# Linear attention with a two-layer PReLU block: batch 0 laid out as 96 partitions of 6 tokens, three stores on another queue, and steps re-placed

## The chip, the cores and the metric

The kernel runs on one core of a Trainium2 chip. The metric is device time in microseconds (us) of one execution; the median of several runs is compared. One execution is also taken by the hardware profiler, and all trace rows come from that one. The engines are TensorE (PE, with its weight loads shown as PEld), VectorE (DVE), ScalarE (ACT), GpSimd (POOL) and SyncE (SP). All of them take their instructions in order. SP, ACT and POOL issue the DMAs.

## The reference

For each of 8 batches and 8 heads (576 tokens, head size 64), linear attention without a softmax, an RMS norm over the head size, and then a two-layer block over all 4608 tokens:

```python
kv = einsum('bhsd,bhse->bhde', k, v)           # 64 x 64 per head
out = einsum('bhsd,bhde->bhse', q, kv)
out = out / sqrt(mean(out * out, -1) + 1e-6) * g_norm
x = out.transpose(0, 2, 1, 3).reshape(4608, 512)
h = x @ w_in                                    # 512 -> 2048
y = (max(h, 0) + alpha * min(h, 0)) @ w_out     # 2048 -> 512
```

Inputs and output are fp32; the kernel computes with fp16 operands and fp32 sums.

## The kernel before

**Blocks and batches.** The 4608 tokens are worked in nine blocks of 512 (`w`), so a block reaches over the edge of a batch of 576. Heads go in four pairs (`j`), since two heads of 64 fill 128 rows. Attention of block `w+1` is computed while block `w` goes through the two-layer block. There are five attention steps per pair. `step_t` transposes q on PE into `qt_ps` and copies it to `qt_sb`. `step_kv` sums k's product with v over the batch's tokens into `kv_ps`, and DVE masks it to `kv_sb`. `step_ot` multiplies the two into `ot_ps`, and ACT squares that. `ssq_mm` sums the squares by a matmul with `mask16`, and ACT makes `rstd`. `norm` (DVE) writes `xt`. `step_ssq` is the last two together.

**Tokens in partitions.** A batch of 576 tokens is loaded as 128 partitions of 4 tokens (`load_main`, fp32 in memory to an fp16 stage `kst`, `qst`, `vst`) and a remainder of 64 tokens (`load_rem`, into `ksb`, `qsb`, `vsb`). Both go through POOL's queue, which casts. The remainder's upper 64 partitions are zeroed once in each of three buffers (`nc.vector.memset(t[nm][REM:P, n - 1, :, :], 0.0)`, line 123), so that all five transposes (line 238) and all five kv matmuls (line 256) of a pair have 128 rows. k and q of the stage are brought into the order of tokens by `regroup` (DVE whole, line 149, or ACT by pairs, `regroup_pair`, line 147).

**Start.** Batch 0 comes in halves. The first four heads of q and k are loaded as fp32 by SP and ACT (`early_half`), cast by DVE and ACT (`cast_pair`, line 520). The rest comes through POOL: three remainders, then v's first half, q's and k's second halves, v's second half, the five pieces of `w_in`, and then batches 1 and 2 and `w_out` in turn. Ten matmuls of `keep_warm` occupy PE until data comes, and three more stand ahead of the first `step_kv`. `alpha_ps` (line 545) transposes the row of alphas in fp32: it is the only matmul with 16 rows.

**Two-layer block.** `m1_group` multiplies `xt` by a column group of `w_in` (four matmuls of 128x512 into one of three banks h0, h1, h2, line 320); `m1_evac` empties the bank by an ACT step (`m_sb`, line 327) and a DVE step (`gt`, line 331), after which it can be filled again. Block 0 multiplies by `w_out` directly (`y_mm`, line 345). Later blocks use a scheme with seven half-size products in place of eight (`prod_mm`, line 468), whose operands are sums of `gt` tiles (`s_sum`) and of weights (`w_sum`). Each block has 16 units `u`, in each of which one `m1_group`, seven products of the block before, and the attention steps due at that unit are issued.

**Order.** The program order of each engine is written out by hand (a manual schedule), so an engine that waits holds everything behind it. Block 2's attention, issued in block 1, follows the table `ATT_1`, all later ones `ATT_AT`. The PSUM tiles come from few banks: h0 to h2, `y`, `s`, `q` and two of `o`; a step waits until its bank's last reader is done. In block 1, ACT copies q of batch 3 in units 12 to 15 (`REG_1`), and k in units 0 and 1 of block 2.

**Stores.** `y_out` copies a finished 128x512 tile to `y_sb` on ACT, and `store_rows` issues its DMA on SP, split where a run of partitions ends.

Of the kernel before, what the change touches and what calls it, by code (L numbers as in the profile page):

```python
# [9 lines left out]
FP32 = mybir.dt.float32  # L10
# [7 lines left out]
def kernel(  # L18
# [11 lines left out]
    nc = tc.nc  # L30
# [12 lines left out]
    REM = S - MAIN  # L43
    NT = TPP + 1
    NF = D_FF // P
    NC = D_MODEL // P
    assert NC == NPAIR and 0 < REM < P
    inv_d = 1.0 / D
# [23 lines left out]

    def early_half(eng, nm, tag):
        st32[nm] = w_p.tile([P, H // 2, TPP * D], FP32, name=f"{nm}32", tag=tag)
        eng.dma_start(
            out=st32[nm][:],
            in_=srcs[nm][0, 0 : H // 2, 0:MAIN, :].rearrange("h (p t) d -> p h (t d)", t=TPP),
        )

    early_half(nc.sync, "q", "wsum2")  # L80
    early_half(nc.scalar, "k", "wsum4")

# [12 lines left out]

    warm16 = const_p.tile([P, W], FP16, name="warm16")
    nc.vector.memset(warm16[:], 0.5)
# [8 lines left out]

    alpha_row = const_p.tile([NF, P], FP32, name="alpha_row")
    nc.sync.dma_start(out=alpha_row[:], in_=moe_alpha[:].rearrange("(g p) -> g p", p=P))
    g2col = const_p.tile([P, 1], FP32, name="g2col")
# [5 lines left out]

    NBUF = 3
    bufs = []
    for i in range(NBUF):
        t = {}
        for nm in ("k", "v", "q"):  # L120
            n = 1 if nm == "v" else NT
            t[nm] = qkv_p.tile([P, n, H, D], FP16, name=f"{nm}sb{i}")
            nc.vector.memset(t[nm][REM:P, n - 1, :, :], 0.0)
        bufs.append(t)
    stages = {}

    def load_main(b, nm, h0, h1):
        st = stages.get((b, nm))
        if st is None:
            st = stage_p.tile([P, H, TPP, D], FP16, name=f"{nm}st", tag=f"{nm}st")  # L130
            stages[b, nm] = st
        nc.gpsimd.dma_start(  # L132
            out=st[:, h0:h1, :, :].rearrange("p h t d -> p h (t d)"),
            in_=srcs[nm][b, h0:h1, 0:MAIN, :].rearrange("h (p t) d -> p h (t d)", t=TPP),
        )
# [15 lines left out]
    def load_batch(b, names=("k", "v", "q")):  # L151
        for nm in names:
            load_rem(b, nm)
            load_main(b, nm, 0, H)

    def regroup_pair(b, nm, j):
        regroup(b, nm, 2 * j, 2 * j + 2, nc.scalar)
# [33 lines left out]

    HH = H // 2
    for nm in ("q", "k", "v"):
        load_rem(0, nm)
    load_main(0, "v", 0, HH)
    load_main(0, "q", HH, H)
    ident = const_p.tile([P, P], FP32, name="ident")
    make_identity(nc, ident[:])
    load_main(0, "k", HH, H)
    load_main(0, "v", HH, H)  # L200
    for i in range(len(IN_CUTS) - 1):
# [21 lines left out]
    qts, kvs, xts = {}, {}, {}  # L223

    def pair_cols(b, nm, j):
        def f(t):
            if nm == "v" and t < TPP:
                return stages[b, nm][:, 2 * j : 2 * j + 2, t, :]
            if nm == "v":
                return bufs[b % NBUF][nm][:, 0, 2 * j : 2 * j + 2, :]  # L230
            return bufs[b % NBUF][nm][:, t, 2 * j : 2 * j + 2, :]
        return f

    def step_t(b, j, pool=(ps_s, "s")):
        qs = pair_cols(b, "q", j)
        qt_ps = pool[0].tile([P, NT * P], FP16, name="qt_ps", tag=pool[1])
        for t in range(NT):
            nc.tensor.matmul(  # L238
                out=qt_ps[:, t * P : (t + 1) * P],
                lhsT=qs(t),  # L240
                rhs=ident16[:],
                is_transpose=True,
                start=(t == 0),
                stop=(t == NT - 1),
            )
        qts[b, j] = attn_p.tile([P, S], FP16, name="qt_sb", tag=f"qt{j}")
        if b == 0:
            nc.vector.tensor_copy(out=qts[b, j][:], in_=qt_ps[:, 0:S])
        else:
            nc.scalar.copy(out=qts[b, j][:], in_=qt_ps[:, 0:S])  # L250

    def step_kv(b, j, pool=(ps_s, "s")):
        ks, vs = pair_cols(b, "k", j), pair_cols(b, "v", j)
        kv_ps = pool[0].tile([P, P], FP32, name="kv_ps", tag=pool[1])
        for t in range(NT):
            nc.tensor.matmul(  # L256
                out=kv_ps[:],
                lhsT=ks(t),
                rhs=vs(t),
                start=(t == 0),  # L260
                stop=(t == NT - 1),
            )
        kvs[b, j] = attn_p.tile([P, P], FP16, name="kv_sb", tag=f"kv{j}")
        nc.vector.tensor_mul(out=kvs[b, j][:], in0=kv_ps[:], in1=mask32[:])  # L264
# [84 lines left out]

    store_engines = [(nc.sync,)]  # L350
    store_turn = [0]

    def store_rows(n0, src, c0, c1):
        i = 0
        while i < P:
            b, r = divmod(n0 + i, S)
            if r < MAIN:
                t, p = divmod(r, P)
                cnt = min(P - i, P - p)
                rows = out[b * S : b * S + MAIN, :].rearrange("(p t) m -> t p m", t=TPP)  # L360
                dst = rows[t, p : p + cnt, c0:c1]
            else:
                cnt = min(P - i, S - r)
                dst = out[b * S + r : b * S + r + cnt, c0:c1]
            engs = store_engines[0]
            store_turn[0] += 1
            engs[store_turn[0] % len(engs)].dma_start(out=dst, in_=src[i : i + cnt])
            i += cnt
# [149 lines left out]

    def cast_pair(nm, st, j, eng_copy):
        eng_copy(  # L520
            out=bufs[0][nm][:, 0:TPP, 2 * j : 2 * j + 2, :].rearrange("p t h d -> p h t d"),
            in_=st[:, 2 * j : 2 * j + 2, :].rearrange("p h (t d) -> p h t d", t=TPP),
        )

    cast_pair("q", st32["q"], 0, nc.vector.tensor_copy)
    cast_pair("k", st32["k"], 0, nc.scalar.copy)
    step_t(0, 0, H_POOL)
    cast_pair("q", st32["q"], 1, nc.vector.tensor_copy)
    cast_pair("k", st32["k"], 1, nc.scalar.copy)
    step_t(0, 1, H_POOL)  # L530
# [4 lines left out]
    step_ot(0, 1)  # L535
    regroup(0, "q", HH, H)
    step_t(0, 2, H_POOL)
    step_t(0, 3, H_POOL)
    regroup(0, "k", HH, H)
    ssq_mm(0, 0, Q_POOL)  # L540
    ssq_mm(0, 1)
    norm(0, 0)
    norm(0, 1)
    alpha_ps = ps_h.tile([P, NF], FP32, name="alpha_ps", tag="h0")
    nc.tensor.matmul(
        out=alpha_ps[:], lhsT=alpha_row[:], rhs=ident[0:NF, 0:NF], is_transpose=True,
        start=True, stop=True,
# [4 lines left out]
    )  # L552
    step_kv(0, 2)
    step_kv(0, 3, Q_POOL)
    step_ot(0, 2)
    step_ot(0, 3, (ps_y, "y"))
# [75 lines left out]
    y_run(1, range(12, 16))  # L632
    y_out(ys[1], 0, 1)
    h_turn[0] = 0
    h_tags[0] = ("h0", "h1", "h2")
# [18 lines left out]
    for what, ats in (  # L654
        ("kv", (1, 2, 3, 4)), ("t", (5, 6, 7, 9)), ("ot", (7, 8, 10, 11)), ("ssq", (9, 10, 12, 13))
    ):
        for j, at in enumerate(ats):
            ATT_1.setdefault(at, []).append((what, j))
    ATT = {"t": step_t, "kv": step_kv, "ot": step_ot, "ssq": step_ssq}

    def attention(w, u):
        if w < NW:
            for what, j in (ATT_1 if w == 2 else ATT_AT).get(u, ()):
                if w < B or what in ("ot", "ssq"):
                    if w == 2 and what in ("kv", "ssq"):
                        pool = O_POOL if what == "kv" and j % 2 else Q_POOL
                        (step_kv if what == "kv" else step_ssq)(w, j, pool)
                    elif w == 2 and what == "ot" and j == 2:
                        step_ot(w, j, (ps_y, "y"))
                    else:  # L670
                        ATT[what](w, j)

    REG_1 = {12 + j: (("q", j),) for j in range(NPAIR)}
    REG_AT = {8 + 2 * j + i: ((nm, j),) for j in range(NPAIR) for i, nm in ((0, "q"), (1, "k"))}

    for w in range(1, NW):
        if w + 2 < B:
            load_batch(w + 2)
        for u in range(NF):
            m1_group(w, G_ORDER[u])  # L680
            if w > 1:
                unit_sums(w, u)
            if w == 1 and u == 4:
                regroup(2, "q", 0, H)
            if w == 2 and u == 0:
# [14 lines left out]
            if w == 1:  # L700
                for k in {7: (0,), 9: (1,), 13: (2,)}.get(u, ()):
                    s_sum(1, 1, k)
                    s_sum(1, 2, k)
            if w + 2 < B:
                for nm, j in (REG_1 if w == 1 else REG_AT).get(u, ()):
                    regroup_pair(w + 2, nm, j)
            if w == 2 and u < 2:
                for j in (2 * u, 2 * u + 1):
                    regroup_pair(3, "k", j)
    w = NW - 1  # L710
    store_engines[0] = (nc.sync, nc.scalar)
# [41 lines left out]
```

## Time and profile before

| | before |
|---|---|
| median of 3 runs (lowest, highest) | 298.6 us (297.7, 299.46) |
| the profiled execution | 297.6 us, of which its span 295.8 us |
| mean granted PE clock | 0.998 |
| PE busy, DVE busy, ACT busy, POOL busy | 95%, 75%, 60%, 16% of the span |
| DMA | busy without a break from about 5 to 75 us, then in pieces |
| HBM read, written | 36.71 MB, 9.44 MB |

A row of a timeline has the start in us, the time in us, engine, line and operation, what is written from what is read, the shape, and in square brackets how long the engine stood idle before it and what ended that. "issue" means that it waited for nothing that the profile shows. Rows of equal instructions are merged (`x5`), and the time is then from the first start to the last end. A matmul's time includes its way through the array, so in a run of them the next starts before the last has ended. Lines with L are lines of the kernel before.

### The profile page before, as it was taken

The numbers are of one execution on the slowest core, as the hardware profiler recorded it, in microseconds if no ns is written. First come the engines' busy times: TensorE is split into PE (matmuls) and PEld (weight loads), VectorE is DVE, ScalarE is ACT, GpSimd is POOL, SyncE is SP. The second block draws the span as 40 slices with busy tenths as digits, with TensorE's granted clock in tenths as the row PEclk, the third lists the DMA queues.
The fourth block names the chain that finished last, engine by engine and source line by source line (L and its number), as shares of the span: only waits on it lengthen the run. The fifth ranks groups of instructions, "written<-read, shape, count | busy, mean of one in ns | idle before, by whom it ended". The sixth has DMA issues, their size and how long they took to land.

```text
span 295.8 us, 5159 instructions
## 1 busy us (share of the span) xinstructions
PE 280.1 (95%) x1970; PEld 179.3 (61%) x1970; DVE 221.5 (75%) x419; ACT 176.1 (60%) x307; POOL 45.9 (16%) x64
## 2 busy tenths in 40 slices
PE   6779999998999999999999999999999999999993
PEld 2434454444666677666666677666666666666782
DVE  6559829679587877797778777877887788787861
ACT  3347367499758856775677668765745565433210
POOL 8644344440203120122002000000000000000000
PEclk9999999999999999999999999999999999999999
DMA  7999999999631990199019401110103011201223
GB/s 159 188 205 198 197 201 193 231 208 192 70 38 39 181 159 5 38 160 161 28 38 136 121 2 35 39 54 21 35 8 100 1 38 35 70 3 37 73 78 100
DMA packets 53081, 28.66 MB, mean 97 GB/s; under 512 B 15152, under 2 KB 52544, under 8 KB 53056
## 3 DMA queue, kind: packets, MB, share of 16 engines
q0 software_dynamic: 41376, 17.83, 48.5%
q1 hardware_dynamic: 10368, 9.32, 10.7%
q10 hardware_dynamic: 1312, 1.18, 1.4%
q8 instruction: 15, 0.25, 0.4%
q14 instruction: 10, 0.08, 0.1%
HBM read 36.71 MB, written 9.44 MB: 156 GB/s over the span
## 4 chain that ended last, share of the span: by engine, by line
PE 69%; DMA 18%; ACT 5%; issue 3%; DVE 2%; POOL 1%; DVEq 0%; POOLq 0%; ACTq 0%
PE h_ps L320 31%; PE yY L468 12%; PE yZ L468 10%; PE yX L468 9%; DMA qst<-in_q_dram 6%; DMA vst<-in_v_dram 5%; DMA w_in_sb<-in_moe_w_in_dram 5%; DMA ksb<-in_k_dram 2%; ACT m_sb L327 2%; PE qt_ps L238 2%; PE ssq_ps L294 2%; PE kv_ps L256 2%; PE ot_ps L278 2%; DVE y_sb L495 1%; ACT ksb L147 1%
## 5 line engine op out<-in xcount | busy, mean ns | idle before, releaser
L320 PE MATMUL h_ps<-xt,w_in_sb 128*128 128x512 f16 x576 | 145.3, 379 | 2.0 <-DVE gt L331 1.8
L331 DVE SCALAR_TENSOR_TENSOR gt<-m_sb,beta_sb,h_ps 128x512 f16<-128x512 f32 x144 | 106.9, 746 | 49.5 <-ACT m_sb L327 47.8
L327 ACT ACTIVATE m_sb<-h_ps 128x512 f32<-128x512 f32 x144 | 86.3, 600 | 65.0 <-PE h_ps L320 50.7
L320 PEld LDWEIGHTS <-w_in_sb 128*128 128x128 f16 x576 | 54.3, 98 | 48.3 <-issue 4.4
L468 PEld LDWEIGHTS <-s 128*128 128x128 f16 x512 | 50.1, 98 | 21.6 <-issue 2.5
L468 PEld LDWEIGHTS <-gt 128*128 128x128 f16 x384 | 37.6, 98 | 14.8
L468 PE MATMUL yY<-wsum,s 128*128 128x256 f16 x256 | 36.3, 273 | 0.0
L468 PE MATMUL yX<-w_out_sb,gt 128*128 128x256 f16 x256 | 35.1, 273 | 0.0
L284 ACT ACTIVATE sq_sb<-ot_ps 128x512 f16<-128x512 f32 x36 | 21.5, 605 | 17.5 <-PE ot_ps L278 17.5
L296 ACT ACTIVATE rstd<-ssq_ps,eps_t 128x512 f32<-128x512 f32 x36 | 24.7, 693 | 9.5 <-PE ssq_ps L294 9.5
L304 DVE SCALAR_TENSOR_TENSOR xt<-ot_ps,g2col,rstd 128x512 f16<-128x512 f32 x36 | 26.5, 745 | 4.2 <-ACT rstd L296 4.2
L250 ACT COPY qt_sb<-qt_ps 128x576 f16<-128x576 f16 x28 | 17.6, 641 | 6.0 <-PE qt_ps L238 6.0
L468 PE MATMUL yZ<-w_out_sb,s 128*128 128x256 f16 x128 | 17.5, 272 | 1.2 <-DVE y_sb L495 1.2
L468 PE MATMUL yY<-wsum,gt 128*128 128x256 f16 x128 | 17.6, 273 | 0.0
L468 PE MATMUL yZ<-wsum,s 128*128 128x256 f16 x128 | 17.6, 273 | 0.0
L345 PE MATMUL y<-w_out_sb,gt 128*128 128x512 f16 x64 | 17.1, 379 | 0.1
L132 POOL DMA_DIRECT2D vst<-in_v_dram x9 | 7.9, 876 | 59.3 <-PE kv_ps L256 52.7
L238 PE MATMUL qt_ps<-ident,qsb 128*128 128x128 f16 x160 | 14.1, 225 | 1.6 <-DVE qsb L520 0.9
L294 PE MATMUL ssq_ps<-sq_sb,mask 128*128 128x512 f16 x36 | 13.5, 379 | 1.4 <-ACT rstd L296 0.7
L278 PE MATMUL ot_ps<-qt_sb,kv_sb 128*128 128x512 f16 (+7 forms) x64 | 13.6, 286 | 0.9 <-DVE kv_sb L264 0.7
L256 PEld LDWEIGHTS <-ksb 128*128 128x128 f16 x160 | 11.6, 100 | 4.1 <-issue 1.3
L238 PEld LDWEIGHTS <-qsb 128*128 128x128 f16 x160 | 10.9, 100 | 5.2 <-DVE qsb L520 1.9
(57 smaller groups left out, 226.1 us busy)
## 6 DMA issues: line engine op xcount, KB each, us to landing
out_dram<-y_sb SPq DMA_DIRECT2D x72, 64.0 KB, 2.1
kst<-in_k_dram POOLq DMA_DIRECT2D x7, 512.0 KB, 12.4
qst<-in_q_dram POOLq DMA_DIRECT2D x7, 512.0 KB, 12.7
vst<-in_v_dram POOLq DMA_DIRECT2D x7, 512.0 KB, 12.7
out_dram<-y_sb SPq DMA_DIRECT2D x23, 128.0 KB, 2.0
w_out_sb<-in_moe_w_out_dram POOLq DMA_DIRECT2D x4, 512.0 KB, 16.5
w_in_sb<-in_moe_w_in_dram POOLq DMA_DIRECT2D x3, 512.0 KB, 12.6
out_dram<-y_sb SPq DMA_DIRECT2D x4, 256.0 KB, 6.9
```

What stands on the lines that cost most here:

```text
L238: nc.tensor.matmul(out=qt_ps[:, t * P : (t + 1) * P], lhsT=qs(t), rhs=ident16[:], is_transpose=True, start=(t == 0), stop=(t == NT - 1),)
L250: nc.scalar.copy(out=qts[b, j][:], in_=qt_ps[:, 0:S])
L256: nc.tensor.matmul(out=kv_ps[:], lhsT=ks(t), rhs=vs(t), start=(t == 0), stop=(t == NT - 1),)
L278: nc.tensor.matmul(out=ot_ps[:, n0 - w * W : n1 - w * W], lhsT=kvs[b, j][:], rhs=qts[b, j][:, n0 - b * S : n1 - b * S], start=True, stop=True,
L284: nc.scalar.activation(out=sq[:], in_=ot_ps[:], func=AF.Square)
L294: nc.tensor.matmul(out=ssq_ps[:], lhsT=mask16[:], rhs=sq[:], start=True, stop=True)
L296: nc.scalar.activation(out=rstd[:], in_=ssq_ps[:], func=AF.Abs_reciprocal_sqrt, bias=eps_t[:], scale=inv_d,)
L304: nc.vector.scalar_tensor_tensor(out=xts[w, j][:], in0=ot_ps[:], scalar=g2col[:], in1=rstd[:], op0=ALU.mult, op1=ALU.mult,)
L320: nc.tensor.matmul(out=h_ps[:], lhsT=w_in_blk(c, g), rhs=xts[w, c][:], start=(c == 0), stop=(c == NC - 1),)
L327: nc.scalar.activation(out=m_sb[:], in_=h_ps[:], func=AF.Relu, scale=-1.0)
L331: nc.vector.scalar_tensor_tensor(out=gts[w, i][:, r, :], in0=m_sb[:], scalar=beta_sb[:, g : g + 1], in1=h_ps[:], op0=ALU.mult, op1=ALU.add,)
L468: nc.tensor.matmul(out=bank, lhsT=lhs, rhs=rhs, start=fresh, stop=(c == NK - 1), skip_group_check=True,)
```

## The change

Batch 0 alone is now cut into 96 partitions of 6 tokens (`P0`, `T0`), which has no remainder: its three `load_rem` go, its q and k first halves are loaded by pairs, its second halves and v come in tiles of their own, and its attention steps make six matmuls of 96 rows where they made five of 128. The upper parts of the remainders of batches 1 to 7 are no longer zeroed; their fifth transpose and fifth kv matmul take the 64 rows that hold data. Block 0's three tiles y0, y2 and y1 are stored from POOL's queue. In the first norm chain `alpha_ps` and `beta_sb` come ahead of the norms, `step_kv(0, 2)` uses an h bank and both kv steps come ahead of the second norm. In block 1 the steps of `ATT_1` are moved, the sums of squares alternate between banks q and s, q of batch 3 is copied by DVE at once in unit 15, and the `s_sum` steps are moved. To make room in SBUF, `warm16` and `alpha_row` share buffers with other tiles.

```diff
+    T0 = next(n for n in range(NT, S) if S % n == 0)
+    P0 = S // T0
...
-    early_half(nc.sync, "q", "wsum2")
-    early_half(nc.scalar, "k", "wsum4")
+    early_pair(nc.sync, "q", 0, "wsum2")
+    early_pair(nc.scalar, "k", 0, "wsum4")
+    early_pair(nc.sync, "q", 1, "wsum1")
+    early_pair(nc.scalar, "k", 1, "wsum3")
...
-    warm16 = const_p.tile([P, W], FP16, name="warm16")
+    warm16 = attn_p.tile([P, W], FP16, name="sq_sb")
...
-    alpha_row = const_p.tile([NF, P], FP32, name="alpha_row")
+    alpha_row = ysb_p.tile([P, D_MODEL], FP32, name="y_sb")
...
-            n = 1 if nm == "v" else NT
+            n = 1 if nm == "v" else T0 if i == 0 else NT
-            nc.vector.memset(t[nm][REM:P, n - 1, :, :], 0.0)
...
-    for nm in ("q", "k", "v"):
-        load_rem(0, nm)
-    load_main(0, "v", 0, HH)
-    load_main(0, "q", HH, H)
+    load_half0("v", 0)
+    load_half0("q", 1)
     ident = const_p.tile([P, P], FP32, name="ident")
     make_identity(nc, ident[:])
-    load_main(0, "k", HH, H)
-    load_main(0, "v", HH, H)
+    load_half0("k", 1)
+    load_half0("v", 1)
...
+    def rows(b, t):
+        return P0 if b == 0 else P if t < TPP else REM
+
+    def n_runs(b):
+        return T0 if b == 0 else NT
...
     def step_t(b, j, pool=(ps_s, "s")):
         qs = pair_cols(b, "q", j)
-        qt_ps = pool[0].tile([P, NT * P], FP16, name="qt_ps", tag=pool[1])
-        for t in range(NT):
+        qt_ps = pool[0].tile([P, S], FP16, name="qt_ps", tag=pool[1])
+        c = 0
+        for t in range(n_runs(b)):
+            n = rows(b, t)
             nc.tensor.matmul(
-                out=qt_ps[:, t * P : (t + 1) * P],
+                out=qt_ps[:, c : c + n],
                 lhsT=qs(t),
-                rhs=ident16[:],
+                rhs=ident16[0:n, 0:n],
...
-    store_engines = [(nc.sync,)]
+    store_engines = [(nc.gpsimd,)]
...
-    regroup(0, "q", HH, H)
+    regroup_half0("q")
     step_t(0, 2, H_POOL)
     step_t(0, 3, H_POOL)
-    regroup(0, "k", HH, H)
+    regroup_half0("k")
     ssq_mm(0, 0, Q_POOL)
     ssq_mm(0, 1)
-    norm(0, 0)
-    norm(0, 1)
     alpha_ps = ps_h.tile([P, NF], FP32, name="alpha_ps", tag="h0")
...
-    step_kv(0, 2)
+    norm(0, 0)
+    step_kv(0, 2, H_POOL)
     step_kv(0, 3, Q_POOL)
+    norm(0, 1)
     step_ot(0, 2)
...
     y_out(ys[1], 0, 1)
+    store_engines[0] = (nc.sync,)
...
-        ("kv", (1, 2, 3, 4)), ("t", (5, 6, 7, 9)), ("ot", (7, 8, 10, 11)), ("ssq", (9, 10, 12, 13))
+        ("kv", (1, 2, 3, 4)), ("t", (6, 7, 8, 9)), ("ot", (8, 9, 11, 12)), ("ssq", (10, 11, 13, 14))
...
-                        pool = O_POOL if what == "kv" and j % 2 else Q_POOL
+                        pool = Q_POOL if j % 2 == 0 else O_POOL if what == "kv" else S_POOL
...
-    REG_1 = {12 + j: (("q", j),) for j in range(NPAIR)}
...
-            if w == 1 and u == 4:
-                regroup(2, "q", 0, H)
+            if w == 1 and u in (4, NF - 1):
+                regroup(2 if u == 4 else 3, "q", 0, H)
...
-                for k in {7: (0,), 9: (1,), 13: (2,)}.get(u, ()):
+                for k in {5: (0,), 8: (1,)}.get(u, ()):
...
+                s_sum(1, u + 1, 2)
```

## The prediction

> **What bounds the kernel now.** I read the page's busy times first, then busy time by stage, then the order of time in the two stages where TensorE (PE) is not full.
>
> ```profile
> span 295.8 us, 5159 instructions
> PE 280.1 (95%) x1970; PEld 179.3 (61%) x1970; DVE 221.5 (75%) x419; ACT 176.1 (60%) x307; POOL 45.9 (16%) x64
> ```
>
> Three stages: the start, most of block 1, and a whole block (columns: stretch and length, then busy time and instructions of PE, PEld, DVE, ACT and POOL, PE's granted clock, DMA share, GB/s).
>
> ```profile
> 2.00:17.90 15.90, 12.00 (x62) 5.64 (x63) 8.97 (x27) 5.37 (x10) 12.24 (x19) 1.00 1.28 200
> 54.00:74.00 20.00, 17.25 (x111) 9.07 (x110) 16.03 (x29) 17.18 (x33) 4.68 (x6) 1.00 1.54 203
> 104.77:135.20 30.43, 30.18 (x230) 20.64 (x228) 24.03 (x46) 21.44 (x38) 4.32 (x6) 1.00 0.65 98
> ```
>
> From 74 us on a block of 512 tokens takes 30.4 us, of which PE is busy 30.2: there PE time alone counts, and any added PE time moves the end one for one. Time can be won only ahead of that: in the start (to 17.9) and in block 1 (54 to 75). The start, in order of time:
>
> ```profile
> 10.47 0.58 PE L256 MATMUL kv_ps<-vst,ksb 128*128 128x128 f16 x4 [0.38 <-DMA vst<-in_v_dram]
> 12.95 0.59 PE L294 MATMUL ssq_ps<-sq_sb,mask 128*128 128x512 f16 x2
> 13.47 0.13 PEld L545 LDWEIGHTS alpha_ps<-ident,alpha_row 16*128 16x128 f32 x1 [0.42 <-issue]
> 13.48 0.23 PE L545 MATMUL alpha_ps<-ident,alpha_row 16*128 16x16 f32 x1
> 14.37 1.39 DVE L304 SCALAR_TENSOR_TENSOR xt<-ot_ps,g2col,rstd 128x512 f16<-128x512 f32 x2
> 15.77 0.47 DVE L264 TENSOR_TENSOR kv_sb<-kv_ps,mask 128x128 f16<-128x128 f32 x2
> ```
>
> And the four stalls of block 1, named in brackets:
>
> ```profile
> 57.62 0.45 PE L238 MATMUL qt_ps<-ident,qsb 128*128 128x128 f16 x5 [0.70 <-DVE qsb L149]
> 65.09 0.38 PE L294 MATMUL ssq_ps<-sq_sb,mask 128*128 128x512 f16 x1 [0.56 <-ACT rstd L296]
> 68.68 0.38 PE L294 MATMUL ssq_ps<-sq_sb,mask 128*128 128x512 f16 x1 [0.19 <-ACT rstd L296]
> 74.20 1.02 PE L320 MATMUL h_ps<-xt,w_in_sb 128*128 128x512 f16 x4 [1.50 <-DVE gt L331]
> ```
>
> **Remainders of batches 1 to 7.** The pads that were zeroed are gone, so the fifth of each run of transposes and of kv matmuls now has 64 rows instead of 128. The built program gives these 56 matmuls (7 batches x 4 pairs x 2) an array tile of 64 rows, and all others 128. So PE changes tile 112 times; before it did so only around alpha. Alpha is the trace's one row for this. The second sum of squares starts at 12.95 + 0.59 - 0.38 = 13.16. Its follower could start 0.215 later (four 128x512 take 0.86 in steady state), at 13.38. Alpha started at 13.48, 0.10 late, though the engine waited for nothing ("issue"). Its weight load, which elsewhere starts some 0.2 us before its matmul, started with it: the load was not taken ahead of the change. I price a change of tile at 0.10 us. Bounds: zero, if alpha was late for being fp32 and not for its rows; 0.165, if PE waits for the last matmul to end (0.219 for one 128x128 transpose against its 0.055 spacing: five take 0.44). I take 0.10 because it is the only row with fewer rows.
> Where it lies: 8 matmuls in batch 1's steps (36 to 42 us, PE back to back) and 40 in blocks 2 to 6, all on the path: 48 x 0.20 = 9.6. The 8 of batch 2 lie in block 1, where ACT and DVE set the pace for half of it: 8 x 0.10 = 0.8. Against that 28 transposes are 64 columns instead of 128: 0.027 each at most, -0.75. Sum +9.65, between -0.75 and about +16.5.
> The Trainium skill, page TensorEngine Tiling (Array Packing), section Key Properties, speaks against this change: it says that switching the tiling mode drains TensorE. It gives no price. If a drain means that a matmul's whole latency is exposed, the sum would be the upper bound above; alpha's 0.10 us is less.
>
> **The start.** The three 64-row loads of batch 0 leave Pool's queue, 0.7 to 0.8 us of issue each, and v's first half is issued first instead of fourth. It landed at 10.34 by its semaphore; I expect some 3 us earlier. But PE then stands in its own queue: ten warm-up matmuls (0.427 apart at the start), a transpose, DVE's copy and second cast, another transpose and three warm-ups end near 10.05, because the cast of 96x768 costs about 0.6 where 128x512 took 0.42. So kv starts 0.4 earlier, not 3. Then 12 kv matmuls instead of 10 at 0.107 each cost 0.2; the copies of q and k from the stage have 1536 elements a partition instead of 1024, 0.42 to 0.63 for q (+0.2) and k with 0.84 now (+0.1 to +0.4, I take 0.1 because k lands earlier). Only one norm (0.70) and beta (0.16) are left ahead of kv_sb: 0.86 where 14.45 to 15.77 was 1.32, -0.5. PE's wait there for rstd to leave bank s goes too, since kv takes an h bank. Sum -0.4, range -1.0 to +0.4. The nine memsets (0.27 each) ended at 4.75, before q landed at 5.81, so nothing comes from them; the identity comes some 2 us earlier on Pool, and nobody waits for it. The buffers that warm16 and alpha_row now share come round again only after their last reader. The split q and k loads are hidden by the warm-ups, which end at 6.5; without that cover a later first cast would cost its lateness.
>
> **Block 1.** The 0.70 goes: q of batch 2 landed at 56.85 with 768 KB of stores beside it and is now asked for a unit later. The waits for rstd (0.56 + 0.19) go: there one sum of squares waited until the one before it had left bank q, and now they alternate banks q and s. ACT loses four copies of 0.62 at units 12 to 15. But the last norm is a unit later, so the next block's first group waits for it: rstd 0.7 after the matmul of unit 14, two DVE steps of 0.75 behind it, 0.6 late. And DVE copies batch 3's q (0.69) just ahead of the evacuation that frees the bank for the second group, so of the 1.50 about 0.9 stays. The third pair of s sums (0.42 each) moves from unit 13 into block 2's units 0 and 1, behind those evacuations; the first two move up a unit or two, where DVE idles. The stalls sum to 2.95; less 0.6 and 0.9 that leaves a gain of 1.45. ACT's 2.5 us of copies shorten its other waits for PE's results a little, and I take -1.7 (from -0.5, if DVE's backlog reaches the norms, to -2.6, if only 0.35 stays).
>
> **Stores on Pool.** Six store issues (about 0.75 each) wait for ACT's three copies of y, at 47.6 to 50. Behind them on Pool stand batch 3's loads, which were issued from 42.9. DMA is not empty for this: what was issued by 41 lasts until q of batch 2 lands, now about 52, and then the stores run. q of batch 3 landed at 68.04 and should land near 65; its copy at unit 15 comes near 68. Cost zero; without that cover DVE, and then PE, would wait the difference.
> The Trainium skill, page DMA: Bandwidth & Descriptors, section Issuing engines are not separate DMA queues, says that DMAs of all issuing engines run on the same 16 engines and interleave, so that moving stores saves issue time only. By it q of batch 2 gains nothing from the move; the 0.70 would still go, by the later unit, and the sum is the same.
>
> **Sum.** +9.65 - 0.4 - 1.7 = +7.55 on the profiled execution's 297.6 (span 295.8), 305.1. The median of the runs, 298.6, is 1.0 above that execution: 306.1, I say 306.
>
> **Rivals.**
> The tile change is free, and the edits do what they are for: -0.75 - 0.4 - 1.7 = -2.85, 295.8 at the median. For it: alpha is fp32, one row, and each 64-row weight load could be hidden as the 128-row ones are. Against: its load had no other reason to be late. It decides below 2.85 / 104 = 0.027 us a change (104 = 48 x 2 + 8). By the ends of the start and block 1, the range is 294 to 297.5.
> A change costs about that, 0.02 to 0.04: within the 0.5% (1.5 us) that a measurement of this kernel can tell from no change.
> A change exposes the whole latency, 0.165: 104 x 0.165 = 17.2, less 2.85, +14.3, 313. Against: alpha's 0.10.
> Pool's queue becomes the bound: batch 3's loads behind the stores. It needs q of batch 3 to land after 68.5, over 3 us later than I reckon, and each us after that is one us of PE. With a free tile change it would eat the 2.85 at a landing of 71.4; 4 us beyond that make 302.6. Against: DMA has the stores themselves to do from 52 to 54, when the first of those loads has long been issued.
>
> **Chances.** Forecast, 0.04 to 0.14 a change: 0.58. Whole latency: 0.06. Pool's queue: 0.02. Break-even: 0.06. Free: 0.28. The forecast's own range is 300 to 311 (104 x 0.04 or x 0.14, less 2.85, on 298.6). The range for 8 in 10 must reach into the free case, since that holds over 0.2: 294.8 to 313. Faster 0.28, same 0.06, slower 0.66.
>
> **What would show it.** In the changed profile blocks 2 to 6 take about 31.9 us each instead of 30.4 (8 x 0.19), and weight loads of the 128x64 transposes and of the next matmul start with their matmul and not ahead. If those blocks keep 30.2 to 30.4, the tile change is free and I am wrong by the whole first term. The first group of block 0 should start at 17.5, the four stalls leave 1.6, and q of batch 2 land near 52. A start at 15 or a block 1 without stalls would show that I under-rated those; a DVE copy of q in unit 15 that waits for a DMA would show Pool's queue.

## The result, and the profile after

| | before | after |
|---|---|---|
| median of 4 runs each (lowest, highest) | 298.62 us (297.7, 299.46) | 306.8 us (306.31, 307.55) |
| the profiled execution | 297.6 us, span 295.8 us | 307.55 us, span 305.8 us |
| mean granted PE clock of the profiled execution | 0.998 | 0.986 |

The ratio after to before is 1.0277, with an interval of 1.024 to 1.0314: slower by 8.2 us at the medians. The page of after, its span, busy times, the granted clock in 40 slices, and the group of transposes:

```profile
span 305.8 us, 5173 instructions
PE 292.5 (96%) x1978; PEld 181.9 (59%) x1978; DVE 220.1 (72%) x411; ACT 174.9 (57%) x303; POOL 46.9 (15%) x67
PEclk9969999999999999999999999999999999999998
L263 PE MATMUL qt_ps<-ident,qsb 128*128 128x128 f16 (+2 forms) x164 | 16.2, 217 | 2.4 <-DVE qsb L167 1.1
```

PE has eight instructions more (1978 for 1970: batch 0's six matmuls per step in place of five), and 12.4 us more busy time, while DVE and ACT have less. "+2 forms" are the transposes of 96 and of 64 rows; they are now one group with the full ones. The third slice of the clock is 6.

The three stretches that the prediction showed of before, now of after (same columns; the third was one whole block of before):

```profile
2.00:17.90 15.90, 12.31 (x71) 5.86 (x72) 6.95 (x18) 6.58 (x10) 10.42 (x16) 0.88 1.20 210
54.00:74.00 20.00, 19.46 (x113) 9.59 (x113) 15.42 (x27) 14.90 (x28) 10.30 (x14) 1.00 1.39 180
104.77:135.20 30.43, 30.18 (x219) 19.93 (x218) 22.84 (x43) 20.84 (x37) 4.72 (x6) 1.00 0.57 84
```

In the last row PE is as full as before (30.18 of 30.43), but the same 30.43 us hold 219 matmuls where they held 230. The stalls of block 1 are mostly filled (19.46 busy for 17.25; over block 1 itself 21.24 of 21.40 us, where before had 20.00 of 21.45), though by matmuls that take longer. In the start the granted clock is 0.88. That column averages the records of the clock that the trace holds, and they begin at 7.12 here and only at 11.50 in the profiled execution of before. Its 1.00 for the start says nothing of the time ahead of 11.50, when PE ran at half speed, as the spacing of its kv matmuls shows, 0.107 us apart in the four at 10.96 (0.63 less the last one's 0.31, by 3), and 0.056 in the four at 14.96:

```profile
10.96 0.63 PE L256 MATMUL kv_ps<-vst,ksb 128*128 128x128 f16 x4
...
14.96 0.39 PE L256 MATMUL kv_ps<-vst,ksb 128*128 128x128 f16 x4
```

Where the time went is read from the first `h_ps` matmul of each block in the order of time (us):

| stretch | before | after | more |
|---|---|---|---|
| to the first group of block 0 | 17.93 | 17.80 | -0.13 |
| block 0, up to the first `y` matmul | 14.66 | 15.77 | +1.11 |
| rest of block 0, with batch 1's attention | 16.57 | 17.84 | +1.27 |
| block 1 | 21.45 | 21.40 | -0.05 |
| block 2 | 32.08 | 33.58 | +1.50 |
| blocks 3 to 5, each | 30.42 | 31.98 | +1.56 |
| block 6 | 30.18 | 31.75 | +1.57 |
| blocks 7 and 8, to the end | 71.69 | 71.68 | 0 |

The start, in order of time, the rows that answer to those of before:

```profile
9.29 0.83 PE L282 MATMUL kv_ps<-vst,ksb 96*128 96x128 f16 x12
...
13.02 0.23 PE L570 MATMUL alpha_ps<-ident,y_sb 16*128 16x16 f32 x1
...
14.25 1.44 PE L282 MATMUL kv_ps<-vst,ksb 96*128 96x128 f16 x12 [1.00 <-DMA vst<-in_v_dram]
...
17.80 2.76 PE L346 MATMUL h_ps<-xt,w_in_sb 128*128 128x512 f16 x6
```

Twelve kv matmuls take 0.83 us at 9.29 and 1.44 at 14.25, and six matmuls of 128x512 take 2.76 us where four in block 3 take 1.04: from 13.95 on PE runs at half its clock. The second kv waits 1.00 us for v's second half.

The whole 10.0 us of span lies where 64-row remainders are, and in the first 15 us of block 0. What one remainder does is seen in the order of time on PE. Before, in block 3:

```profile
109.99 0.44 PE L238 MATMUL qt_ps<-ident,qsb 128*128 128x128 f16 x5
110.27 1.03 PE L320 MATMUL h_ps<-xt,w_in_sb 128*128 128x512 f16 x4
...
111.90 0.39 PE L256 MATMUL kv_ps<-vst,ksb 128*128 128x128 f16 x4
112.12 0.22 PE L256 MATMUL kv_ps<-vsb,ksb 128*128 128x128 f16 x1
112.12 0.37 PEld L320 LDWEIGHTS <-w_in_sb 128*128 128x128 f16 x3
112.18 0.59 PE L320 MATMUL h_ps<-xt,w_in_sb 128*128 128x512 f16 x2
```

The same after:

```profile
108.02 0.52 PE L263 MATMUL qt_ps<-ident,qsb 128*128 128x128 f16 x5
108.47 1.04 PE L346 MATMUL h_ps<-xt,w_in_sb 128*128 128x512 f16 x4
...
110.11 0.39 PE L282 MATMUL kv_ps<-vst,ksb 128*128 128x128 f16 x4
110.43 0.23 PE L282 MATMUL kv_ps<-vsb,ksb 64*128 64x128 f16 x1
110.59 0.55 PEld L346 LDWEIGHTS <-w_in_sb 128*128 128x128 f16 x4
110.59 1.04 PE L346 MATMUL h_ps<-xt,w_in_sb 128*128 128x512 f16 x4
```

From the first of four kv matmuls to the remainder's it is 0.32 instead of 0.22 (+0.10), from the remainder's to the next matmul 0.16 instead of 0.06 (+0.10). From five transposes to what follows it is 0.45 instead of 0.28. The weight load behind the remainder starts with its matmul (both 110.59), where before it started 0.06 ahead of it (112.12 and 112.18). No engine is named as the cause in brackets, and PE counts as busy throughout: this cost is not in the view of waits at all, only in the spacing of starts.

Block 1's waits after, PE alone:

```profile
64.11 0.52 PE L263 MATMUL qt_ps<-ident,qsb 128*128 128x128 f16 x5 [0.16 <-ACT qt_sb L276]
...
74.42 0.38 PE L346 MATMUL h_ps<-xt,w_in_sb 128*128 128x512 f16 x1 [0.79 <-DVE xt L330]
```

The four stalls of before are gone from the brackets of PE. In their place are a wait of 0.16 us for `qt_sb` and the late norm of the prediction (0.79 for an expected 0.6).

### The profile page after: what moved, and what is told of

The parts are those of the page before. It is cut to its first block, busy times and chain, and to the rows that moved or that the text cites. A ratio compares the mean times of both kernels' runs of the same rounds, so it can differ in the third digit from the quotient of the medians.

```text
span 305.8 us, 5173 instructions
## 1 busy us (share of the span) xinstructions
PE 292.5 (96%) x1978; PEld 181.9 (59%) x1978; DVE 220.1 (72%) x411; ACT 174.9 (57%) x303; POOL 46.9 (15%) x67
## 4 chain that ended last, share of the span: by engine, by line
PE 81%; ACT 5%; DVE 5%; DMA 3%; issue 3%; POOL 1%; DVEq 0%; ACTq 0%; POOLq 0%
PE h_ps L346 36%; PE yY L495 12%; PE yZ L495 9%; PE yX L495 9%; PE kv_ps L282 4%; PE y L371 4%; DMA vst<-in_v_dram 3%; PE qt_ps L263 3%; PE ssq_ps L320 2%; ACT m_sb L353 2%; PE ot_ps L304 2%; DVE gt L357 2%; ACT sq_sb L310 1%; DVE y_sb L522 1%; ACT ksb L157 1%
## 5 line engine op out<-in xcount | busy, mean ns | idle before, releaser
L346 PE MATMUL h_ps<-xt,w_in_sb 128*128 128x512 f16 x576 | 147.5, 383 | 1.2 <-DVE xt L330 0.8
L346 PEld LDWEIGHTS <-w_in_sb 128*128 128x128 f16 x576 | 52.8, 98 | 49.3 <-issue 3.3
L322 ACT ACTIVATE rstd<-ssq_ps,eps_t 128x512 f32<-128x512 f32 x36 | 24.5, 690 | 10.5 <-PE ssq_ps L320 10.4
L276 ACT COPY qt_sb<-qt_ps 128x576 f16<-128x576 f16 x28 | 17.5, 638 | 6.2 <-PE qt_ps L263 6.1
L495 PE MATMUL yZ<-w_out_sb,s 128*128 128x256 f16 x128 | 17.5, 272 | 1.2 <-DVE y_sb L522 1.2
L263 PE MATMUL qt_ps<-ident,qsb 128*128 128x128 f16 (+2 forms) x164 | 16.2, 217 | 2.4 <-DVE qsb L167 1.1
L263 PEld LDWEIGHTS <-qsb 128*128 128x128 f16 (+2 forms) x164 | 11.9, 99 | 8.9 <-DVE qsb L547 1.5
L282 PEld LDWEIGHTS <-ksb 128*128 128x128 f16 (+2 forms) x164 | 13.0, 100 | 6.4 <-DVE beta_sb L575 1.1
L142 POOL DMA_DIRECT2D vst<-in_v_dram x7 | 6.2, 890 | 61.7 <-PE kv_ps L282 56.2
L290 DVE TENSOR_TENSOR kv_sb<-kv_ps,mask 128x128 f16<-128x128 f32 x32 | 9.1, 285 | 7.4 <-PE kv_ps L282 7.3
```

The lines of the kernel that those rows point to most:

```text
L263: nc.tensor.matmul(out=qt_ps[:, c : c + n], lhsT=qs(t), rhs=ident16[0:n, 0:n], is_transpose=True, start=(t == 0), stop=(t == n_runs(b) - 1),)
L276: nc.scalar.copy(out=qts[b, j][:], in_=qt_ps[:])
L282: nc.tensor.matmul(out=kv_ps[:], lhsT=ks(t), rhs=vs(t), start=(t == 0), stop=(t == n_runs(b) - 1),)
L322: nc.scalar.activation(out=rstd[:], in_=ssq_ps[:], func=AF.Abs_reciprocal_sqrt, bias=eps_t[:], scale=inv_d,)
L346: nc.tensor.matmul(out=h_ps[:], lhsT=w_in_blk(c, g), rhs=xts[w, c][:], start=(c == 0), stop=(c == NC - 1),)
L495: nc.tensor.matmul(out=bank, lhsT=lhs, rhs=rhs, start=fresh, stop=(c == NK - 1), skip_group_check=True,)
```

## The experiments

My theory was that 112 changes of PE's array tile are the whole loss, that the steps of block 1 gain 1 to 2 us against it, and that the stores and the start do nothing. Rivals: that the loss is due to the placed steps, to the stores on POOL's queue, or to the number of 64-row matmuls rather than to changes between them. In the diffs below `+` is the experiment. The kernel before had a median of 297.6 us in these runs, and each ratio is against that.

**All of the change but the 64 rows (pad128).** The pads are zeroed again and every remainder is taken in 128 rows.

```diff
-        return P0 if b == 0 else P if t < TPP else REM
+        return P0 if b == 0 else P
...
+            if i > 0 or nm == "v":
+                nc.vector.memset(t[nm][REM:P, n - 1, :, :], 0.0)
...
+    for nm in ("q", "k"):
+        nc.vector.memset(bufs[0][nm][REM:P, TPP, :, :], 0.0)
```

> The changed kernel with one thing undone: the fifth transpose and kv matmul of batches 1 to 7 have 128 rows again, over zeroed pads (batch 0 keeps 96 x 6; the pads of the first buffer are zeroed by two DVE steps of 0.27 us in block 0). Theory: the 112 changes of PE's tile are the whole loss. In the changed profile a 64-row transpose starts 0.152 us after its predecessor and the next matmul 0.133 after it, where 0.055 each is normal (+0.175), for kv 0.152 and 0.159 (+0.20). 28 of each are 10.5 us, of which the 8 of block 1 count by half: about -9.7, so 297 us (296.3 to 297.8), and 30.2 to 30.4 us for a block. Rival: the loss comes from the start, where PE ran at half rate until 20.8 us, or from POOL's queue; then this stays above 304.

Measured 296.26 us (295.66 to 297.51), ratio 0.9953 (0.9931 to 0.9976): 10.5 us less than after, and faster than before. A block in its middle, PE's busy time as before again, and its count but for one:

```profile
104.77:135.20 30.43, 30.18 (x231) 20.60 (x229) 24.01 (x45) 21.45 (x39) 4.72 (x6) 1.00 0.66 97
```

So the 64-row remainders are the whole loss, and the rest of the change is a small gain.

**The 64 rows alone, in the kernel before (before_64).** Transposes and kv matmuls of the remainder take `[0:64]`, in all eight batches (64 matmuls); both conditions in the first line below are always true.

```diff
+            n = P if t < TPP else REM if (nm == "q" and True) or (nm != "q" and True) else P
...
-            return bufs[b % NBUF][nm][:, t, 2 * j : 2 * j + 2, :]
+            return bufs[b % NBUF][nm][0:n, t, 2 * j : 2 * j + 2, :]
...
-                rhs=ident16[:],
+                rhs=ident16[0 : min(P, S - t * P), 0 : min(P, S - t * P)],
```

> The kernel before with that one part alone: its remainders' transposes and kv matmuls in 64 rows (transposes 64 columns wide), for all 8 batches, 64 matmuls in place of 56. Theory of the tile change: +10 to +11 us, 308.5 to 310. Rival (64 rows cost nothing, narrower transposes even save up to 0.027 us each): 297.8 to 298.6.

Measured 310.03 us (307.13 to 310.38), ratio 1.0377 (1.0325 to 1.0428). Blocks 3 to 5 take 31.98 us, the figure of after. It needs no other part of the change. The median is raised by the clock of the start (below): three of the four executions had a mean granted clock of 0.973 to 0.983 and took 309.75 to 310.38 us, the fourth had 0.996 and took 307.13, 9.5 more than before.

**The 64 rows in the kv matmuls alone (before_64kv).** As above, with 128 rows for the transposes.

> The kernel before with 64 rows in the 32 remainders of kv alone; the transposes keep 128. Half of the tile changes of before_64, which was 12.4 us over before. Theory: about half, 303 to 304 (32 x 0.20 = 6.4 less what the start hides). Rival: only transposes are dear, then 298; or only kv, then 309.

Measured 302.84 us (302.61 to 304.67), ratio 1.0181 (1.0153 to 1.021). Block 3 of this kernel, from its first group to the next block's, and then block 3 of before_64:

```profile
104.38:135.63 31.25, 31.01 (x231) 20.79 (x229) 24.02 (x46) 21.43 (x39) 4.72 (x6) 1.00 0.62 90
```

```profile
105.95:137.94 31.99, 31.74 (x231) 20.91 (x229) 24.02 (x46) 21.44 (x39) 4.72 (x6) 1.00 0.61 90
```

The same 231 matmuls take 30.18 us of PE with none of 64 rows (pad128's row above), 31.01 with four, 31.74 with eight. A kv remainder costs 0.83 / 4 = 0.21, a transposed one 0.73 / 4 = 0.18, the difference being the 64 columns that it saves (0.027). Both are two changes of 0.10.

**Is it the change, or the 64-row matmul (after_twice)?** After each 64-row transpose of the changed kernel stands a second one of the same data, into spare columns: 28 matmuls of 64 rows more, and no change of tile more.

```diff
+        runs = list(range(n_runs(b))) + ([TPP] if b else [])
-        for t in range(n_runs(b)):
+        for i, t in enumerate(runs):
```

> The changed kernel, in which each of the 28 transposes with 64 rows is followed by a second one that writes the same columns into 64 spare ones of the bank (nobody reads them). Twice as many 64-row transposes, the same number of changes of PE's tile. Theory (the price is that of the change): 28 x 0.03 to 0.06 us, so +0.8 to +1.7, 307.6 to 308.5. Rival (the price is that of a 64-row matmul, 0.175 each): +4.9, 311.7.

Measured 308.01 us (307.33 to 308.16), ratio 1.0337 (1.0316 to 1.0358): 1.2 us more than after. In a whole block it is 0.12 us for four:

```profile
105.66:137.76 32.10, 31.86 (x234) 21.00 (x232) 24.01 (x46) 21.44 (x39) 4.72 (x6) 1.00 0.59 87
```

Blocks 3 to 5 go from 31.98 to 32.10, 0.03 us for each added matmul, which is what 64 columns take (0.027). Had each paid two changes, it would have been four times 0.2. The price stands on the change between 128 and 64 rows.

**Fewer rows, but over 64 (pad96_warm).** Remainders in 96 rows, 32 of them zeros, in the version with filler matmuls that comes below.

```diff
-        return P0 if b == 0 else P
+        return P0 if b == 0 else P if t < TPP else 96
```

> Remainders of batches 1 to 7 in 96 rows (64 with data, 32 of zeros) in place of the 128 of the kernel with filler matmuls. Theory (what costs is the array tile of 64 rows; 96 rows keep the tile of 128): blocks 3 to 6 take 30.4 us or a little less, since the fifth transpose is 32 columns narrower (28 x 0.0135 = 0.4 us in all), and the time is 295.7 to 296.2. Rival (any matmul with other rows than the one before it pays 0.10 us, coming and going): blocks 3 to 6 take 32.0 us, and the time is about 306.

Measured 295.9 us (295.49 to 296.25), ratio 0.9933 (0.9913 to 0.9953). The groups of kv matmuls in blocks 3 to 6, with the form of the remainder at the end, and a whole block:

```profile
L285 PE MATMUL kv_ps<-vst,ksb x61: 219/219/219, 104.8 to 213.4; 128*128 128x128 f16 x61
L285 PE MATMUL kv_ps<-vsb,ksb x16: 221/221/222, 104.9 to 213.5; 96*128 96x128 f16 x16
```

```profile
104.24:134.67 30.43, 30.18 (x231) 20.59 (x229) 24.04 (x46) 21.48 (x39) 4.79 (x7) 1.00 0.66 98
```

Blocks 3 to 5 take 30.40 us. A remainder of 96 rows costs nothing, so it is not "fewer rows than before" that costs: something that 64 rows bring with them and 96 do not, which fits the smaller tile of the prediction. The trace shows rows and not tiles. The median is the lowest of all versions, though not clear of the 296.11 with 128 rows.

**The stores back on SP (pad128_sp)**, the rest as pad128.

```diff
-    store_engines = [(nc.gpsimd,)]
+    store_engines = [(nc.sync,)]
```

> As pad128, with block 0's three stores back on SP. Theory: the stores' queue is worth nothing, since q of batch 2 is needed a unit later: within 0.5 us of pad128. Rival: with the stores beside it q of batch 2 lands some 3 us later (53.5 with the stores on POOL) and unit 6 of block 1 waits for it: up to 1 us slower. Second rival: batch 3's loads, which stood behind the stores until 54, come earlier and free DVE's copy of q in unit 15: up to 1 us faster.

Measured 296.46 us (296.25 to 297.99), ratio 0.9965 (0.9946 to 0.9983), against pad128's 296.26: the queue of the stores is worth nothing that can be measured.

**Block 1's steps back (pad128_blk1)**, the rest as pad128. The old places of the steps, banks, copies of q by ACT, and `s_sum` steps.

```diff
-        ("kv", (1, 2, 3, 4)), ("t", (6, 7, 8, 9)), ("ot", (8, 9, 11, 12)), ("ssq", (10, 11, 13, 14))
+        ("kv", (1, 2, 3, 4)), ("t", (5, 6, 7, 9)), ("ot", (7, 8, 10, 11)), ("ssq", (9, 10, 12, 13))
...
-                        pool = Q_POOL if j % 2 == 0 else O_POOL if what == "kv" else S_POOL
+                        pool = O_POOL if what == "kv" and j % 2 else Q_POOL
...
-            if w == 1 and u in (4, NF - 1):
-                regroup(2 if u == 4 else 3, "q", 0, H)
+            if w == 1 and u == 4:
+                regroup(2, "q", 0, H)
...
+    REG_1 = {12 + j: (("q", j),) for j in range(NPAIR)}
...
-                for k in {5: (0,), 8: (1,)}.get(u, ()):
+                for k in {7: (0,), 9: (1,), 13: (2,)}.get(u, ()):
...
-                s_sum(1, u + 1, 2)
```

> As pad128, with block 1 as before: the old places of transposes, ot and sums of squares, all sums of squares in bank q, q of batch 3 copied by ACT in four pieces, the old places of the s sums. Theory: the re-placed steps are worth 1.7 us (0.5 to 2.6), so 298.7 where pad128 has 297. Rival: they only move the waits; then equal to pad128.

Measured 297.63 us (296.64 to 298.16), ratio 0.999 (0.9973 to 1.0008). At the medians the placed steps are worth 1.4 us. Some of that goes with the clock in the start (below): six of its ten executions had a mean granted clock of 0.988 or less, three of pad128's seven. Between the four executions of each at 0.991 or above it is 1.0 (297.2 and 296.2), and blocks 1 and 2 of the two profiles differ by 0.7, 53.43 us here and 52.76 in pad128. The waits of PE in pad128's block 1:

```profile
60.42 0.44 PE L266 MATMUL qt_ps<-ident,qsb 128*128 128x128 f16 x5 [0.34 <-ACT qt_sb L279]
70.50 0.38 PE L349 MATMUL h_ps<-xt,w_in_sb 128*128 128x512 f16 x1 [0.86 <-DVE xt L333]
72.42 1.02 PE L349 MATMUL h_ps<-xt,w_in_sb 128*128 128x512 f16 x4 [0.20 <-DVE gt L360]
```

and in the kernel with the old places:

```profile
58.07 0.46 PE L266 MATMUL qt_ps<-ident,qsb 128*128 128x128 f16 x5 [0.50 <-DVE qsb L161]
65.53 0.38 PE L323 MATMUL ssq_ps<-sq_sb,mask 128*128 128x512 f16 x1 [0.56 <-ACT rstd L325]
69.13 0.38 PE L323 MATMUL ssq_ps<-sq_sb,mask 128*128 128x512 f16 x1 [0.19 <-ACT rstd L325]
74.73 1.02 PE L349 MATMUL h_ps<-xt,w_in_sb 128*128 128x512 f16 x4 [1.50 <-DVE gt L360]
```

The old waits go as planned, and others come. Counted as the excess of each start-to-start gap over the columns' time, the four old waits cost 3.4 us; six new ones cost 2.8 (0.51 at 60.42, 1.02 at 70.50, then 0.29, 0.36 and 0.30 up to 76.1, and 0.29 at 50.9).

**PE's clock in the start (pad128_warm, after_warm).** Five filler matmuls of 128x512 after the first two `step_ot`, and five after the first norm, in a bank that is free, as `keep_warm` has them already.

```diff
+    keep_warm(5, (ps_y, "y"))
     regroup_half0("q")
...
     norm(0, 0)
+    keep_warm(5, (ps_y, "y"))
     step_kv(0, 2, H_POOL)
```

> As pad128, with five matmuls of 128x512 into the idle bank y after the first two ot steps and five after alpha, where PE stood idle 1.0 and 1.4 us in pad128. Theory: the granted clock, which went from full to half at 14.2 us and came back at 17.6 (pad128) or 20.8 (the changed kernel), now stays full from about 7 to 11 us on; first group of block 0 by 16.6 in place of 17.3, and the median 1.0 lower (0.5 to 2), 295.3. Rival: the landing of v's second half (14.0) and the chain behind it set the start whatever the clock; then it stays at 296.3.

Measured 296.11 us (295.82 to 296.65), ratio 0.9945 (0.9928 to 0.9963): 0.15 less than pad128. The gain is not in the median, since most executions of pad128 had little to lose. Of its seven, four had a mean granted clock of 0.991 and above and took 295.66 to 296.26; three had 0.986 and took 297.06 to 297.51. Of pad128_sp's ten, six at 0.991 and above took 296.25 to 296.49, four at 0.988 and below 297.36 to 297.99. All six with fillers had 0.996 or more. The four of after had 0.984 to 0.986, without exception. Before falls too, but seldom: of its 44 executions beside the experiments eight had 0.982 to 0.989. So the question was put to after itself:

> The changed kernel itself with ten filler matmuls in the start, so that PE's granted clock does not fall to half around 14 to 21 us. Theory (the fall costs the start and the first units of block 0 some 1.2 us, as the executions with a mean clock of 0.986 and below differ from the others in the kernels with 128 rows): first group of block 0 at 17.3 or earlier, mean clock 0.99 or more, time 305.4 to 305.8 (306.8 - 1.2). Rival (the landing of v's second half at 14.1 and the chain behind it set the start whatever the clock): first group at 17.8, time 306.5 to 307.

Measured 305.57 us (305.34 to 305.95), ratio 1.0259 (1.0237 to 1.0282), 1.2 us less than after, as expected. Three stretches of the start, first of after, then of after_warm (columns as above, the clock being third from the end):

```profile
10.53:13.95 3.42, 1.64 (x17) 0.83 (x16) 2.07 (x6) 2.13 (x4) 1.57 (x2) 1.00 1.35 200
13.95:20.77 6.82, 6.34 (x23) 2.67 (x24) 3.16 (x6) 2.65 (x5) 3.33 (x5) 0.50 1.30 204
20.77:24.18 3.41, 3.41 (x17) 1.57 (x16) 1.85 (x3) 2.10 (x4) 0.69 (x1) 1.00 1.38 198
```

```profile
10.53:13.95 3.42, 3.32 (x26) 1.55 (x26) 1.98 (x6) 2.03 (x4) 1.47 (x2) 1.00 1.34 200
13.95:20.77 6.82, 6.03 (x34) 2.62 (x33) 3.42 (x7) 3.44 (x7) 3.42 (x5) 1.00 1.30 204
```

In after PE is busy for 1.64 of the 3.42 us up to 13.95, and then runs at half its clock for 6.82: 23 matmuls there, 34 with fillers. With them the first group of block 0 starts at 17.25 instead of 17.80, and from there to the first `y` matmul it is 14.66 us instead of 15.77. The fillers show that PE's idle time here is what loses the clock. How much of it is too much is not shown. Taken in steps of 3.41 us from the first record of the clock, as after's own steps lie, before kept its clock behind two stretches in which PE was busy for 68% and 61%:

```profile
11.50:14.91 3.41, 2.32 (x22) 1.32 (x21) 2.66 (x6) 2.36 (x4) 1.81 (x3) 1.00 1.45 195
14.91:18.32 3.41, 2.07 (x15) 0.93 (x13) 1.33 (x5) 1.74 (x4) 2.09 (x3) 1.00 1.33 205
```

and pad128_sp lost it behind one with 61%:

```profile
11.52:14.93 3.41, 2.08 (x20) 0.99 (x19) 2.78 (x7) 2.39 (x4) 1.90 (x2) 1.00 1.38 198
14.93:21.76 6.83, 6.65 (x25) 2.64 (x24) 2.65 (x5) 2.43 (x4) 3.08 (x4) 0.50 1.27 205
```

**Two of block 1's remaining waits (pad128_best).** The last sum of squares a unit earlier, and the banks of block 2 started with the other one.

```diff
-        ("kv", (1, 2, 3, 4)), ("t", (6, 7, 8, 9)), ("ot", (8, 9, 11, 12)), ("ssq", (10, 11, 13, 14))
+        ("kv", (1, 2, 3, 4)), ("t", (6, 7, 8, 9)), ("ot", (8, 9, 11, 12)), ("ssq", (10, 11, 12, 13))
...
                 h_tags[0] = ("h1", "h2")
+                h_turn[0] = 1
```

> As pad128_warm, with two small steps in block 1 in which pad128's stalls were 0.86 and 0.60 us: the last two sums of squares one unit earlier (12 and 13), so that the next block's first group need not wait for the last norm, and the second group of block 2 takes bank h1, not again h2. Theory: -0.5 to -1.2 against pad128_warm, 294.5. Rival: ACT and DVE are the pace there, and the wait only moves: equal to pad128_warm.

Measured 296.13 us (295.66 to 296.23), ratio 0.9939 (0.9922 to 0.9957): the same as pad128_warm. PE's waits in block 1 and the first units of block 2:

```profile
67.20 0.38 PE L323 MATMUL ssq_ps<-sq_sb,mask 128*128 128x512 f16 x1 [0.20 <-ACT sq_sb L313]
71.80 0.45 PE L266 MATMUL qt_ps<-ident,qsb 128*128 128x128 f16 x5 [0.78 <-DVE qsb L161]
76.18 0.28 PE L498 MATMUL yY<-wsum,s 128*128 128x256 f16 x1 [0.49 <-DVE s L450]
```

The wait for `xt` at 70.5 is gone, and the transposes of q of batch 3 now wait for DVE's copy of it, one us later. DVE has the norms, the evacuations and that copy to do in this stretch, whatever comes first. A miss.

## Why the prediction was right, and where it was not

**The remainders, +9.65: right.** The cleanest pair is after_warm against pad128_warm, which differ in the rows alone and both keep a full clock in the start. Summed over the rest of block 0 and blocks 1 to 6 their profiles differ by 1.20 + 0.98 + 1.18 + 1.56 + 1.56 + 1.58 + 1.57 = 9.63 us, and their medians by 305.57 - 296.11 = 9.46. The price of 0.10 us a change came from one row, alpha's, and holds: 0.096 us from 128 rows to 64, 0.10 back, by the gaps between starts. Blocks 3 to 5 took 31.98 us where 31.9 was said. The cheap rival (a free change) would have needed 30.2 to 30.4 there, the dear one (a whole latency of 0.165) 33.0. Block 2, which the prediction's sign took in, went from 32.08 to 33.58: the 30.4 was never its time. Two things were luck. Alpha's row, in fp32 and with 16 rows, showed only the way in, and the way back was taken to cost the same. And the agreement to 0.02 us is a sum of misses that cancel: 1.20 in the rest of block 0 and 1.18 in block 2 where the prediction's terms make 1.5 each, against 0.98 in block 1 for 0.7, and 1.57 in each full block for 1.5.

What the Trainium skill says on the page TensorEngine Tiling (Array Packing), section Key Properties, that a change of tiling mode drains TensorE, agrees with these runs: a late matmul, and a weight load that does not start ahead. The page gives no price; here it is 0.10 us, less than the 0.16 that a matmul's latency exceeds its spacing by.

**The start, -0.4: wrong.** The step that failed is the one that took PE's clock as given: a chain with less PE work in it can lose the clock. Half speed from 13.95 to 20.77 cost 1.11 us in block 0, and 0.55 ahead of it: the first group started at 17.80 for an expected 17.5, and with fillers at 17.25, though v's second half landed 0.3 later there. The prediction also left out the wait for v's second half, which landed at 14.11 (14.39 before) and held the second kv for 1.00 us. Together the start came to -0.13 + 1.11 = +0.98 instead of -0.4, a miss of 1.4.

The other steps of this sum can't be judged by one pair of profiles. Kv started at 9.29 for an expected 10.05, but the prediction reckoned with the half speed that PE had up to 11.50 in before, and in the profiled execution of after it had full speed from 7.12 on. The start of pad128_sp is the same but for the zeroed pads, and its record of the clock begins at 11.52; there kv started as the prediction had it:

```profile
8.61 1.48 PE L231 MATMUL warm_ps<-sq_sb,mask 128*128 128x512 f16 x3
10.15 1.44 PE L285 MATMUL kv_ps<-vst,ksb 96*128 96x128 f16 x12
```

The three warm-ups end at 10.09, and kv starts 0.32 ahead of before's 10.47, near the 0.4 that was said (v's first half had landed at 9.96, so it may have been the limit as well). V's first half landed at 8.78 in after, 1.6 us earlier than before and not 3. What the new start gains while the clock holds lies between nothing and 0.4 us: its first group started at 16.78 in pad128_warm and at 17.25 in after_warm, where v's second half landed at 13.92 and 14.39, and the old start's at 17.21 in before_64kv, with full speed from 5.19 and four 64-row matmuls in the way.

**Block 1, -1.7: mis-sized.** The mechanism was right in the parts that the changed profile shows: the waits for q and `rstd` went, and the late norm came at 0.79 for 0.6. But the step "that leaves a gain of 1.45" counted only the stalls in brackets and two successors. With remainders in 128 rows the steps gain 53.43 - 52.76 = 0.67 us in blocks 1 and 2 (against before, 53.53, 0.77). By the gaps between starts the four old stalls were worth 3.4 and not 2.95, and the two foreseen successors 1.02 + 0.36 = 1.38 for 1.5. What was left out is four small waits, 0.29 at 50.9, 0.51 at 60.4, 0.29 at 71.8 and 0.30 at 76.1, together 1.4 us, which the brackets show as 0.34 or less or leave out. 3.4 - 1.38 - 1.39 is the 0.6 that was gained.

**The stores, 0: right.** POOL's six issues ran from 50.76 and their data landed from 54.0 to 56.1; q of batch 2 landed at 53.50 (expected near 52, before 56.85), and q of batch 3 at 67.70 (near 65, before 68.04), still ahead of its copy at 74.94. Nobody waited for POOL's queue, and with SP in its place the time is the same.

**The sum.** 9.63 + 0.98 - 0.7 = 9.9 on the profiled execution, which measured +10.0 of span; predicted was +7.55. At the medians it is +8.2, nearer to the prediction, because the runs of before in that comparison were slower (298.6) than those beside the experiments (297.6). Against 297.6 the change costs 9.2. That the median came within 0.8 us of the 306.0 is in part luck for that reason: by the terms the prediction was 2.4 us short, 1.4 in the start and 1.0 in block 1.

## What to carry to other kernels

Rows of zeros cost nothing here: on a full PE a remainder of 64 rows was cheaper as 96 or 128 rows with a zeroed pad, because a 64-row matmul among 128-row ones paid about 0.2 us for the two changes and saved 0.03 at most. Where such matmuls can't be padded, putting them next to one another is worth a try: for two transposes it saved the second pair of changes. Work that is taken out of PE's path in a chain of waits can cost more than it saves if PE's granted clock falls for it: look at the clock by stage after such an edit, and fill the gaps. When steps are re-placed in a stage that several engines almost fill, count the gap between starts and not the stalls in brackets, since stalls of 0.3 us come back in numbers.

## What the runs showed of the hardware

- A change between matmuls of 128 rows and of 64 costs about 0.10 us each way (0.096 in, 0.10 out), as busy time without a wait; alpha's 16 rows came 0.10 late too. 96 rows cost nothing (30.40 us a block with them, 30.42 with 128). Where between 64 and 96 the edge lies was not tried, nor whether two 64-row matmuls of different kinds side by side share one pair of changes, though two transposes do. Whether the 0.10 is PE emptying itself or the weight load that starts late is not separated: the trace shows both at once.
- PE's clock fell to half without PE having been idle for long: the longest gap between 10.53 and 13.95 was 1.07 us (ahead of the transposes at 11.97), and PE was busy for 1.64 of 3.42 us. It stayed at half for 6.82 us though PE was busy for 6.34 of them. The Trainium skill, page TensorE: Matmul & The Clock Gate, Part 1, tells of free-running windows of about 3.4 us after which the clock is set; the steps at 13.95, 20.77 and the 7.12 before them, 6.83 and 6.82 apart, agree with two such windows each. It names an idle window as what lowers the clock; here a window that was half busy did. What share holds it stays open, and PE's busy time alone does not settle it: 2.07 of 3.41 us held in before, and 2.08 did not in pad128_sp. Pad128's profiled execution fell at 14.21, behind 1.62 of 3.41, while another execution of that kernel kept a mean of 0.999.
- When the clock first rises and when data lands differ between executions: the clock's record begins between 5.16 and 11.52 us in the twelve profiles, and v's second half landed at 13.83 in pad128 and at 14.70 in pad128_sp, whose start is the same code. Their first groups started at 17.33 and 18.33.
- Executions of one kernel with a mean granted clock of 0.988 or less took 1.0 to 1.3 us (0.4%) more than its others (pad128: 297.2 and 296.2; pad128_sp: 297.7 and 296.4), as much as the re-placed steps are worth. With ten filler matmuls no execution of the four kernels that have them fell below 0.995.
